# Loading k ahead of q, and the weights in column halves, in a channel-attention plus maxout kernel

## The chip, the cores and the metric

The kernel runs on one core of one Trainium2 chip. The metric is the device time of one execution in microseconds (us). Each kernel was run several times; a "run" below is one execution. All runs quoted here are of the state called fast (none is marked slow in the record). The profile is a trace of one execution; its span is about 1.8 us shorter than the run time of that execution.

The engines: PE is TensorE (matmul), PEld its weight loads, DVE is VectorE, ACT is ScalarE, POOL issues the loads that cast, SP issues the stores.

## The reference

Four batches. In each, a 256 x 256 attention matrix is formed between channels, over 6144 tokens, and the result goes through a maxout layer:

```python
# q, k, v: [4, 6144, 256] fp32, tau = 1
qn = q / (norm(q, axis=1) + 1e-6);  kn = k / (norm(k, axis=1) + 1e-6)   # norms over the tokens
a  = softmax(kn.transpose(0, 2, 1) @ qn / tau)                          # [4, 256, 256]
x  = (v @ a).reshape(24576, 256)
h  = maximum(maximum(x @ w1, x @ w2), x @ w3)                           # w: [256, 768]
out = h @ w_out                                                         # [24576, 256] fp32
```

The kernel never forms v @ a. It folds the attention matrix into the weights (A^T W, a [256, 768] matrix for each of w1 to w3 and each batch) and multiplies v by that.

## The kernel before

Per batch: *gram* multiplies q by k, and also q by q and k by k, whose diagonals are the squared norms; *softmax_t* makes `et`, the unnormalised exponentials; *rowsums* and *aw_half* make A^T W in two column halves; then 12 chunks of 512 tokens follow, each of six blocks (three matmul pairs, then a maximum over the three results by ACT and DVE) and four output steps. Batch b+1's gram stands before the last chunk of batch b, its softmax after the first block (block 0) of that chunk.

```python
alloc_qk(0)
for w in [2, 2] + [4] * 10 + [2, 2]:          # batch 0: q and k alternate, fp32 -> fp8 on the way
    load_qk(0, g0, w); g0 += w                # a piece of width w is w*256 values on each of 128 partitions
for i, w in enumerate(w_list):                # then w1, w2, w3 whole, v(0), v(1), w_out, v(2)
    ...
def gram(b):                                  # one pass over q and k
    ps = [xtile(f"gram{j}") for j in range(CC)]           # CC = 2
    for tp in range(NG // 2):                             # 24 steps
        for j in range(CC):
            PE.matmul(ps[j][:, 0:C],           lhsT=q_j, rhs=k, ...)       # fp8 DoubleRow
            PE.matmul(ps[j][:, C:C + P],       lhsT=q_j, rhs=q_j, ...)
            PE.matmul(ps[j][:, C + P:C + 2*P], lhsT=k_j, rhs=k_j, ...)
    return ps
def softmax_t(ps):
    dkm = ps's k.k blocks * identity                      # DVE, 2 instructions
    PE.matmul(kb_ps, lhsT=ones_f, rhs=dkm)                # k's norms, to all partitions, fp32
    n2q = diagonal sums of ps's q.q blocks                # DVE
    lnk, rkb = Ln(kb_ps), Exp(-0.5 * lnk)                 # ACT: 1 / norm of k
    lnq, rq  = Ln(n2q), Exp(-0.5 * lnq)                   # ACT: 1 / norm of q
    for j in range(CC):
        e_in = ps[j][:, 0:C] * rkb                        # DVE
        et[:, j, :] = Exp(e_in * rq[:, j])                # ACT
...
aw_half(et, rinv, aw, 0); v_transpose(0); aw_half(et, rinv, aw, 1)    # batch 0, ahead of chunk 0
```

(`htile` takes one of six PSUM buffers, which the blocks use too; `xtile` one of two, for gram, transposes and output.)

## Time and profile before

| | before |
|---|---|
| median of the first runs | 631.12 us (630.97 to 632.14) |
| the profiled execution | 629.19 us, span 627.3 us |
| PE busy | 598.0 us, 95% |
| q and k of batch 0 all landed | 36.6 us |

The table of engines on the page of the kernel before (busy us, share of the span, instructions):

```profile
PE 598.0 (95%) x3960; PEld 371.3 (59%) x3960; DVE 409.9 (65%) x638; ACT 287.6 (46%) x529; POOL 69.8 (11%) x134
```

PE is nearly always busy, so time can only be won where PE waits or does needless work. The view of waits, for PE alone (who waited for whom: us in total, times, longest), says where it waits:

```profile
PE gram L148 <- DMA k_sb<-in_k_dram: 14.8, 12, 5.2
PE kb_ps L163 <- DVE dkm L160: 5.9, 4, 1.8
...
PE h_ps L240 <- ACT s_mx L243: 0.8, 3, 0.3
PE vt_ps L226 <- DMA v_sb<-in_v_dram: 0.5, 1, 0.5
```

The 14.8 us are the loading of batch 0. The kb_ps wait is the softmax: one of 0.4 us at the start and one of 1.8 us at each of three batch boundaries. Both places are seen in the timeline (start us, length us, engine, line, operation, out<-in, count, and in brackets the idle time before it and what ended that). This is the start, from the landing of the last k; rows of weight loads and a few others are left out:

```profile
36.59 0.27 PE L148 MATMUL gram<-k_sb,q_sb 128*128 128x512 fp8e4 x1 [0.26 <-DMA k_sb<-in_k_dram]
...
37.09 0.49 DVE L160 TENSOR_TENSOR dkm<-gram,ident 128x128 f32<-128x128 f32 x2 [36.08 <-PE gram L152]
...
37.63 0.70 PE L163 MATMUL kb_ps<-dkm,ones_f 128*128 128x256 f32 x2 [0.41 <-DVE dkm L160]
...
38.37 0.38 ACT L171 ACTIVATE lnk<-kb_ps 128x256 f32<-128x256 f32 x1 [36.35 <-PE kb_ps L163]
...
39.23 0.75 DVE L180 TENSOR_TENSOR e_in<-gram,rkb 128x256 f32<-128x256 f32 x2 [1.11 <-ACT rkb L172]
...
39.76 0.91 ACT L181 ACTIVATE et<-e_in,rq 128x256 bf16<-128x256 f32 x2 [0.23 <-DVE e_in L180]
...
40.81 2.17 PE L205 MATMUL ew_ps<-w_sb,et 128*128 128x384 bf16 x12
```

From the landing at 36.59 us to the first ew_ps matmul at 40.81 (A^T W) there are 4.2 us of a chain that runs through DVE, PE, ACT, DVE and ACT again. Later, v_transpose of chunk 1, which stands between blocks 0 and 1, began at 47.18 us. The next lines are PE at the first batch boundary. The gram before them began at 162.28:

```profile
174.26 1.47 PE L240 MATMUL h_ps<-vt_sb,aw_sb 128*128 128x512 bf16 x6
177.56 0.67 PE L163 MATMUL kb_ps<-dkm,ones_f 128*128 128x256 f32 x2 [1.83 <-DVE dkm L160]
...
181.09 1.51 PE L240 MATMUL h_ps<-vt_sb,aw_sb 128*128 128x512 bf16 x6 [0.27 <-ACT s_mx L243]
182.44 0.82 PE L259 MATMUL o_ps<-wo_sb,ht_sb 128*128 128x256 bf16 x6
```

Block 0 of the last chunk (6 matmuls) is followed by a wait of 1.83 us for dkm, then kb_ps, then blocks 1 and 2 (left out), a wait of 0.27, block 3, and at 182.44 an output step. From 174.26 to 182.44 PE does 5.2 us of block matmuls (24 at 0.216) in 8.18 us.

The view of windows gives, for a stretch, PE busy, granted clock, the busy share of the DMA engines and the GB/s written:

```profile
3.00:10.00 7.00, 2.06 (x12) 1.00 1.05 77
12.00:28.00 16.00, 12.51 (x80) 1.00 1.12 105
```

The DMA engines are full. (Their share is a mean over 16 engines and reads above 1 in both stretches, so the GB/s say more about the speed.) Since fp32 becomes fp8, 105 GB/s written is about 420 GB/s read (an estimate, 4 x 105).

### The profile page before, as it was taken

Reading aid. Unit: us, or ns where it says so; the run is one execution under the profiler, and the core shown is the slowest. Engines: PE = TensorE matmul, PEld = TensorE weight load, DVE = VectorE, ACT = ScalarE, POOL = GpSimd, SP = SyncE. Lnnn points to the kernel's source line nnn. Section 1 sums busy time; section 2 is a strip of 40 time slices with the busy share of each in tenths; the row PEclk is TensorE's granted clock in tenths of the full one; section 3 lists DMA queues with packets and bytes.
Section 4 is the critical chain, followed back from the end, with each engine's and each line's share of the span. In section 5 each row is a group of like instructions: output and inputs, shape, how many; then the busy total and the mean of one; then the engine's idle time right before and its main releaser. Section 6 shows DMA issues by size and latency. Waiting matters only on the chain. (4 is left out here: it accounts for less than half of the span.)

```text
span 627.3 us, 10335 instructions
## 1 busy us (share of the span) xinstructions
PE 598.0 (95%) x3960; PEld 371.3 (59%) x3960; DVE 409.9 (65%) x638; ACT 287.6 (46%) x529; POOL 69.8 (11%) x134
## 2 busy tenths in 40 slices
PE   3779999999989999999989999999998999999996
PEld 3755555555855555555676555555585555565554
DVE  0038777777366877777716877777736677777774
ACT  0045554555146555454416554454514655545452
POOL 6432111100002212100001211110000000000000
PEclk9999999999999999999999999999999999999999
DMA  8999676513009676722204857652300431311011
GB/s 72 105 182 131 116 107 117 96 51 102 35 1 150 99 97 121 106 86 67 85 1 71 122 111 109 119 94 59 93 34 1 101 69 50 100 53 68 35 67 68
DMA packets 26418, 52.58 MB, mean 84 GB/s; under 512 B 2816, under 2 KB 14080, under 8 KB 26368
## 3 DMA queue, kind: packets, MB, share of 16 engines
q0 software_dynamic: 19456, 26.75, 36.4%
q1 hardware_dynamic: 6912, 25.17, 10.2%
q8 instruction: 31, 0.51, 0.3%
q14 instruction: 19, 0.16, 0.1%
HBM read 78.64 MB, written 25.17 MB: 165 GB/s over the span
## 5 line engine op out<-in xcount | busy, mean ns | idle before, releaser
L240 PE MATMUL h_ps<-vt_sb,aw_sb 128*128 128x512 bf16 x1728 | 410.2, 379 | 0.8 <-ACT s_mx L243 0.8
L244 DVE TENSOR_TENSOR s_mx<-h_ps,s_mx 128x512 bf16<-128x512 f32 x288 | 197.9, 687 | 130.5 <-ACT s_mx L243 130.5
L240 PEld LDWEIGHTS <-aw_sb 128*128 128x128 bf16 x1728 | 167.0, 98 | 157.0 <-issue 2.2
L243 ACT ACTIVATE s_mx<-h_ps 128x512 bf16<-128x512 f32 x288 | 171.4, 596 | 162.4 <-PE h_ps L240 162.4
L245 DVE TENSOR_TENSOR ht_sb<-h_ps,s_mx 128x512 bf16<-128x512 f32 x288 | 199.3, 692 | 30.0
L259 PE MATMUL o_ps<-wo_sb,ht_sb 128*128 128x256 bf16 x1152 | 155.4, 273 | 0.9 <-DVE ht_sb L245 0.9
L259 PEld LDWEIGHTS <-ht_sb 128*128 128x128 bf16 x1152 | 112.7, 98 | 51.9 <-DVE ht_sb L245 1.1
L262 ACT ACTIVATE o_sb<-o_ps 128x512 f32<-128x512 f32 x96 | 57.3, 597 | 91.4 <-PE o_ps L259 88.8
L108 POOL DMA_DIRECT2D v_sb<-in_v_dram x48 | 25.7, 535 | 469.5 <-PE vt_ps L226 366.3
L148 PE MATMUL gram<-k_sb,q_sb 128*128 128x512 fp8e4 x192 | 55.7, 327 | 14.8 <-DMA k_sb<-in_k_dram 14.8
L229 ACT ACTIVATE vt_sb<-vt_ps 128x512 bf16<-128x512 bf16 x96 | 52.1, 594 | 34.8 <-PE vt_ps L226 34.8
L152 PE MATMUL gram<-k_sb 128*128 128x256 fp8e4 x192 | 46.6, 243 | 0.0
L150 PE MATMUL gram<-q_sb 128*128 128x256 fp8e4 x192 | 46.2, 241 | 0.0
L150 PEld LDWEIGHTS <-q_sb 128*128 128x256 fp8e4 x192 | 27.8, 145 | 9.6 <-issue 9.3
L226 PEld LDWEIGHTS <-v_sb 128*128 128x128 bf16 x384 | 25.4, 98 | 11.3 <-DMA v_sb<-in_v_dram 0.9
L148 PEld LDWEIGHTS <-q_sb 128*128 128x256 fp8e4 x192 | 27.7, 144 | 6.3 <-DMA q_sb<-in_q_dram 5.9
L152 PEld LDWEIGHTS <-k_sb 128*128 128x256 fp8e4 x192 | 30.2, 157 | 0.0
L226 PE MATMUL vt_ps<-ident,v_sb 128*128 128x128 bf16 x384 | 29.3, 219 | 0.5 <-DMA v_sb<-in_v_dram 0.5
L160 DVE TENSOR_TENSOR dkm<-gram,ident 128x128 f32<-128x128 f32 x8 | 1.9, 281 | 36.1 <-PE gram L152 36.1
L171 ACT ACTIVATE lnk<-kb_ps 128x256 f32<-128x256 f32 x4 | 1.5, 384 | 44.6 <-PE kb_ps L163 44.6
L100 POOL DMA_DIRECT2D k_sb<-in_k_dram x38 | 20.8, 548 | 9.6 <-DMA k_sb<-in_k_dram 7.2
L99 POOL DMA_DIRECT2D q_sb<-in_q_dram x38 | 20.7, 544 | 6.2 <-DMA q_sb<-in_q_dram 6.1
(27 smaller groups left out, 78.4 us busy)
## 6 DMA issues: line engine op xcount, KB each, us to landing
out_dram<-o_sb SPq DMA_DIRECT2D x48, 512.0 KB, 2.6
v_sb<-in_v_dram POOLq DMA_DIRECT2D x48, 256.0 KB, 3.6
q_sb<-in_q_dram POOLq DMA_DIRECT2D x24, 192.0 KB, 5.4
k_sb<-in_k_dram POOLq DMA_DIRECT2D x24, 192.0 KB, 6.9
q_sb<-in_q_dram POOLq DMA_DIRECT2D x10, 128.0 KB, 9.7
k_sb<-in_k_dram POOLq DMA_DIRECT2D x10, 128.0 KB, 9.7
w_sb<-in_moe_w_dram POOLq DMA_DIRECT2D x3, 384.0 KB, 8.0
wo_sb<-in_moe_w_out_dram POOLq DMA_DIRECT2D x1, 384.0 KB, 11.2
```

The source lines that it names most:

```text
L108: POOL.dma_start(out=t, in_=v_r[gi // NCH, gi % NCH])
L148: PE.matmul(ps[j][:, 0:C], lhsT=qt[:, tsl, jsl], rhs=kt[:, tsl, :], start=(tp == 0), stop=last, perf_mode=DR, skip_group_check=True)
L150: PE.matmul(ps[j][:, C:C + P], lhsT=qt[:, tsl, jsl], rhs=qt[:, tsl, jsl], start=False, stop=last, perf_mode=DR, skip_group_check=True)
L152: PE.matmul(ps[j][:, C + P:C + 2 * P], lhsT=kt[:, tsl, jsl], rhs=kt[:, tsl, jsl], start=False, stop=last, perf_mode=DR, skip_group_check=True)
L226: PE.matmul(vt_ps[:, i * P:(i + 1) * P], lhsT=v_sb[:, t, cc * P:(cc + 1) * P], rhs=ident, is_transpose=True, start=(i == 0), stop=(i == CC ...
L229: ACT.activation(out=vt[:, cc, :], in_=vt_ps[:, cc * CHUNK:(cc + 1) * CHUNK], func=AF.Copy)
L240: PE.matmul(t, lhsT=aw[m][:, ic, fsl], rhs=vt[:, ic, :], start=(ic == 0), stop=(ic == CC - 1))
L243: ACT.activation(out=s_mx, in_=hp[0], func=AF.Copy)
L244: DVE.tensor_tensor(out=s_mx, in0=hp[1], in1=s_mx, op=ALU.max)
L245: DVE.tensor_tensor(out=ht[:, fc, :], in0=hp[2], in1=s_mx, op=ALU.max)
L259: PE.matmul(st["ps"][:, half], lhsT=ht[:, fc, t * P:(t + 1) * P], rhs=wo_sb[:, fc, :], start=(fc == 0), stop=(fc == FC - 1))
L262: ACT.activation(out=st["o"][:, t - 1:t + 1, :].rearrange("p t d -> p (t d)"), in_=st["ps"], func=AF.Copy)
```

## The change

The intent: k's norms need only k. If k is loaded whole ahead of q, k.k and its whole chain (dkm, kb_ps, lnk, rkb) run while q is still arriving, and only q's norms are left when the last q lands. Weights come in halves, so that the first half of A^T W can start sooner, and v(0) comes between the halves; the second half of A^T W moves behind block 0 of chunk 0. The gram function is shared, so later batches change too: the k.k pass comes first, and dkm, kb_ps, lnk, rkb run inside gram.

```diff
-    for w in [2, 2] + [4] * 10 + [2, 2]:
-        load_qk(0, g0, w)
+    for load, widths in ((load_k, [4, 4] + [8] * 5), (load_q, [8] * 5 + [4, 2, 2])):
+        ...  # the identity is made after the second k piece instead of before the first
-    (w1, w2, w3 whole), load_v(0), load_v(1)
+    load_w(0); load_v(0); load_w(1); load_v(1)          # column halves
 def gram(b):
+        kk = htile("kk")
+        for tp in range(NG // 2):
+            for j in range(CC):
+                PE.matmul(kk[:, jsl], lhsT=k_j, rhs=k_j, ...)
+        dkm = kk * identity                              # DVE
         for tp in range(NG // 2):
             for j in range(CC):
                 PE.matmul(q_j, k) ; PE.matmul(q_j, q_j)
-                PE.matmul(k_j, k_j)
+            if tp == 11:
+                kb_ps (PE), lnk, rkb (ACT)
-def softmax_t(ps):      # dkm, kb_ps, n2q, lnk, rkb, lnq, rq, e_in, et
+def softmax_t(ps, rkb): # n2q, lnq, rq, e_in, et
...
     v_transpose(0)
-    aw_half(et, rinv, aw, 1)
...
+            if gi == 0:
+                gaps[0].insert(0, lambda: aw_half(et, rinv, aw, 1))   # after block 0 of chunk 0
```

More of the change, by code (lines that the diff above doesn't have):

```diff
@@ L95, in alloc_qk, with load_k, load_q @@
                  qk_pool.tile([P, NG, C], FP8, name="k_sb", tag="k"))
-    def load_qk(b, g0, w):
-        qt, kt = qk[b]
-        POOL.dma_start(out=qt[:, g0:g0 + w, :], in_=q_r[b][:, g0:g0 + w, :])
-        POOL.dma_start(out=kt[:, g0:g0 + w, :], in_=k_r[b][:, g0:g0 + w, :])
+    def load_k(b, g0, w):
+        POOL.dma_start(out=qk[b][1][:, g0:g0 + w, :], in_=k_r[b][:, g0:g0 + w, :])
+    def load_q(b, g0, w):
+        POOL.dma_start(out=qk[b][0][:, g0:g0 + w, :], in_=q_r[b][:, g0:g0 + w, :])
     v_tiles = {}
@@ L109, in load_v, with load_w @@
         v_tiles[gi] = t
-    ident = consts.tile([P, P], BF16, name="ident")
-    make_identity(nc, ident)
     alloc_qk(0)
-    g0 = 0
-    for w in [2, 2] + [4] * 10 + [2, 2]:
-        load_qk(0, g0, w)
-        g0 += w
-    w_sb = []
-    for i, w in enumerate(w_list):
-        wt = consts.tile([P, CC, d_ff], BF16, name=f"w{i}_sb")
-        POOL.dma_start(out=wt, in_=w.rearrange("(cc p) f -> p cc f", p=P))
-        w_sb.append(wt)
+    for load, widths in ((load_k, [4, 4] + [8] * 5), (load_q, [8] * 5 + [4, 2, 2])):
+        g0 = 0
+        for w in widths:
+            load(0, g0, w)
+            g0 += w
+            if load is load_k and g0 == 8:
+                ident = consts.tile([P, P], BF16, name="ident")
+                make_identity(nc, ident)
+    w_sb = [consts.tile([P, CC, d_ff], BF16, name=f"w{i}_sb") for i in range(3)]
+    def load_w(fh):
+        fsl = slice(fh * FH, (fh + 1) * FH)
+        for wt, w in zip(w_sb, w_list):
+            POOL.dma_start(out=wt[:, :, fsl], in_=w.rearrange("(cc p) f -> p cc f", p=P)[:, :, fsl])
+    load_w(0)
     load_v(0)
+    load_w(1)
     load_v(1)
@@ L141, in gram @@
         qt, kt = qk[b]
+        kk = htile("kk")
+        for tp in range(NG // 2):
+            tsl = slice(2 * tp, 2 * tp + 2)
+            for j in range(CC):
+                jsl = slice(j * P, (j + 1) * P)
+                PE.matmul(kk[:, jsl], lhsT=kt[:, tsl, jsl], rhs=kt[:, tsl, jsl], start=(tp == 0 and j == 0),
+                          stop=(tp == NG // 2 - 1), perf_mode=DR, skip_group_check=True)
+        dkm = sm.tile([P, C], FP32, name="dkm")
+        for j in range(CC):
+            jsl = slice(j * P, (j + 1) * P)
+            DVE.tensor_tensor(out=dkm[:, jsl], in0=kk[:, jsl], in1=ident, op=ALU.mult)
         ps = [xtile(f"gram{j}") for j in range(CC)]
@@ L151, in gram @@
                           start=False, stop=last, perf_mode=DR, skip_group_check=True)
-                PE.matmul(ps[j][:, C + P:C + 2 * P], lhsT=kt[:, tsl, jsl], rhs=kt[:, tsl, jsl],
-                          start=False, stop=last, perf_mode=DR, skip_group_check=True)
-        return ps
-    def softmax_t(ps):
-        dkm = sm.tile([P, C], FP32, name="dkm")
-        for j in range(CC):
-            DVE.tensor_tensor(out=dkm[:, j * P:(j + 1) * P], in0=ps[j][:, C + P:C + 2 * P],
-                              in1=ident, op=ALU.mult)
-        kb_ps = htile("kb_ps")
-        PE.matmul(kb_ps[:, :C], lhsT=ones_f, rhs=dkm, start=True, stop=True)
+            if tp == 11:
+                kb_ps = htile("kb_ps")
+                PE.matmul(kb_ps[:, :C], lhsT=ones_f, rhs=dkm, start=True, stop=True)
+                lnk = sm.tile([P, C], FP32, name="lnk")
+                rkb = sm.tile([P, C], FP32, name="rkb")
+                ACT.activation(out=lnk, in_=kb_ps[:, :C], func=AF.Ln)
+                ACT.activation(out=rkb, in_=lnk, func=AF.Exp, scale=-0.5)
+        return ps, rkb
+    def softmax_t(ps, rkb):
         n2q = sm.tile([P, CC], FP32, name="n2q")
@@ L168, in softmax_t @@
                                      op0=ALU.mult, op1=ALU.add, accum_out=n2q[:, j:j + 1])
-        lnk = sm.tile([P, C], FP32, name="lnk")
-        rkb = sm.tile([P, C], FP32, name="rkb")
-        ACT.activation(out=lnk, in_=kb_ps[:, :C], func=AF.Ln)
-        ACT.activation(out=rkb, in_=lnk, func=AF.Exp, scale=-0.5)
         lnq = sm.tile([P, CC], FP32, name="lnq")
@@ L268, in o_steps @@
         return [lambda t=t: step(t) for t in range(TPC)]
-    ps = gram(0)
-    et = softmax_t(ps)
+    et = softmax_t(*gram(0))
     aw = alloc_aw()
@@ L288 @@
             if more and 1 <= ch < 9:
-                load_qk(b + 1, (ch - 1) * 6, 6)
+                load_k(b + 1, (ch - 1) * 6, 6)
+                load_q(b + 1, (ch - 1) * 6, 6)
             gaps = [[] for _ in range(FC)]
@@ L301 @@
                 if ch == NCH - 1 and more and fc == 0:
-                    et = softmax_t(ps)
+                    et = softmax_t(*ps)
                 for f in gaps[fc]:
```

## The prediction

> **What bounds the kernel now.** TensorE. Engine table: PE busy 598 of 627.3 us (95%), DVE 65%, ACT 46%. The waits view lists only about 25 us for PE, nearly all in two places: 14.8 us for k_sb while batch 0's q and k arrive (0 to 37 us), and each batch's softmax: 5.9 us for dkm before the kb_ps matmul (0.4 us at the start, 1.8 us at each of three batch boundaries), 2.2 us for et, 0.5 us for v_sb. So the change can only act on the start and three boundaries.
>
> **The start** is bound by DMA: from 12 to 28 us the windows view shows 104 to 105 GB/s written with the engines full. Fp32 becomes fp8, so about 418 GB/s is read (estimate)[...]. The bytes are the same, so k ahead of q doesn't shorten the stream. It ends earlier because the identity is no longer ahead of the first issue (1.42 us, to about 0.75: 0.7 us), and perhaps because the 2-wide pieces leave the front, where only about 80 GB/s was written from 3 to 10 us (estimate 0 to 1 us). The last k lands at 36.6 us; I expect the last q at about 35.4.
>
> After that landing, the timeline before shows: gram's end, dkm 37.1, kb_ps 37.6, lnk 38.4, rkb to 39.2, e_in, et from 39.8, first ew_ps 40.8, h_ps of block 0 from 45.9 to 47.2: landing + 10.6. After, dkm to rkb are done during q's arrival; left are n2q (0.6), lnq, rq (0.4), et: ew_ps at landing + 2.7 instead of + 4.2. v(0) lands before the second weight half, so the 0.5 us wait goes. But the second half of A^T W, moved behind block 0, no longer fills PE during the vt_sb copies (1.08 us on ACT): 0.7 to 1 us comes back as a new wait of h_ps for vt_sb. Block 0 plus both halves end at about landing + 9.8. Start in all: 1.2 + 0.8 = 2.0 us.
>
> PE clock: triples of gram matmuls took 0.44 us until 35.6 us, then 0.25[...].
>
> **Each boundary.** Gram has the same 144 matmuls and weight loads. The 1.8 us dkm wait goes, and lnk/rkb (0.8 us) leave ACT's chain. But the next blocks' PSUM then waits for ACT, which runs et before s_mx: from block 0 to the end of block 3 I work out 6.6 us instead of 8.2. kb_ps (0.5) moves into gram. Net 0.9 us each, 2.7 in all; gram could grow by 0.5 us each where weight loads bind (0.08 us apart, warm).
>
> **Prediction.** 631.1 - 2.0 - 2.7 = 626.4 us; 8 in 10 between 623.0 and 629.2. Faster by over 2%: 0.02; within 2%: 0.97; slower: 0.01.
>
> **Shown right or wrong by:** last q landing near 35.4; ew_ps near landing + 2.7; a new h_ps wait for vt_sb; at boundaries no dkm wait but an h_ps wait for s_mx of 1.4 us instead of 0.3; gram at 12 us per batch.
>
> **Wrong if:** PE is cold and behind q; wide pieces stream faster or slower; the kk pass is bound by weight loads; DVE is late with dkm.

Two passages are cut, and the cuts are marked. Neither held a term of the sum, which stands as recorded: 631.1 - 2.0 - 2.7 = 626.4 us. One compared the estimated 418 GB/s with a figure that no run of this case shows; the other explained the change from 0.44 to 0.25 us, and expected from that explanation that PE would keep up with q; no run of this case shows it. "Cold" and "warm" are only names for the wider and the closer spacing of gram's matmuls.

## The result, and the profile after

| | before | after |
|---|---|---|
| median | 631.05 us (630.47 to 632.14, 4 runs) | 624.96 us (624.64 to 625.25, 4 runs) |
| ratio, with 95% interval | | 0.9901 (0.9884 to 0.9919) |
| the profiled execution: run time, span | 629.19, 627.3 | 624.64, 622.8 |

A ratio here is the mean time of one kernel's fast runs over that of the other's of the same rounds, so it is not quite the ratio of the medians.

The change gains 1%, about 6.1 us by the medians; that is clear of the noise. But the two profiles differ by only 4.5 us. That gap is itself a finding, taken up below.

PE's waits after the change:

```profile
PE kk L154 <- DMA k_sb<-in_k_dram: 13.7, 7, 5.2
PE h_ps L253 <- ACT s_mx L256: 3.5, 3, 1.2
PE gram L166 <- DMA q_sb<-in_q_dram: 2.5, 3, 1.2
...
PE h_ps L253 <- ACT vt_sb L242: 0.7, 1, 0.7
```

The dkm wait is gone, as intended. In its place stand a wait of h_ps for s_mx, about 1.2 us at each of the three boundaries, and one of 0.7 us for vt_sb at the start. The start after the change, from the landing of the last q (rows left out as before):

```profile
35.04 0.32 PE L166 MATMUL gram<-k_sb,q_sb 128*128 128x512 fp8e4 x1
...
36.12 0.75 DVE L193 TENSOR_TENSOR e_in<-gram,rkb 128x256 f32<-128x256 f32 x2
...
36.70 0.91 ACT L194 ACTIVATE et<-e_in,rq 128x256 bf16<-128x256 f32 x2
...
37.77 3.62 PE L218 MATMUL ew_ps<-w_sb,et 128*128 128x384 bf16 x12
...
42.52 1.73 PE L253 MATMUL h_ps<-vt_sb,aw_sb 128*128 128x512 bf16 x5 [0.69 <-ACT vt_sb L242]
...
44.08 2.11 PE L218 MATMUL ew_ps<-w_sb,et 128*128 128x384 bf16 x12
...
46.03 0.61 PE L239 MATMUL vt_ps<-ident,v_sb 128*128 128x128 bf16 x8
```

The last q lands at 35.04 us instead of 36.59, and the first ew_ps starts 2.73 us after it instead of 4.2. So far, that is 3.0 us won. But then 12 ew_ps matmuls take 3.62 us, where they took 2.17 before. The windows view (columns as above: PE busy with its count, granted clock, DMA share, GB/s) shows why:

```profile
36.00:37.00 1.00, 0.00 (x0) 1.00 1.32 212
...
37.40:37.60 0.20, 0.04 (x1) 0.61 1.06 196
37.60:40.60 3.00, 2.94 (x12) 0.50 1.26 199
```

PE idled from 35.6 to 37.27 us, and from about 37.4 to 40.9 us its granted clock was 0.50. The mark, v_transpose of chunk 1 (the last line of the timeline above), is at 46.03 us, only 1.15 us earlier than before; it now has block 0 and all of A^T W behind it, as it had before. What halved the clock this profile alone doesn't show; experiment 3 tests the idle gap before it, and experiments 2 and 4 show that the outcome changes from run to run.

At the first boundary, where gram began at 161.13 us:

```profile
173.81 3.83 PE L253 MATMUL h_ps<-vt_sb,aw_sb 128*128 128x512 bf16 x17
178.83 1.51 PE L253 MATMUL h_ps<-vt_sb,aw_sb 128*128 128x512 bf16 x6 [1.18 <-ACT s_mx L256]
180.18 0.82 PE L272 MATMUL o_ps<-wo_sb,ht_sb 128*128 128x256 bf16 x6
```

Blocks 0 to 2 run in one piece (the trace has 17 of their 18 matmuls), and block 3 waits 1.18 us. Blocks 0 to 3 now take 6.37 us (173.81 to 180.18) instead of 8.18. Gram takes 12.68 us instead of 11.98, mostly since kb_ps is inside it. From the start of gram to the end of block 3 it is 19.05 instead of 20.16 us: 1.11 us less. The other two boundaries show the same (19.04 instead of 20.16, 19.05 instead of 20.15), so the three give 3.3 us.

The stream of loads:

```profile
3.00:10.00 7.00, 1.49 (x8) 1.00 1.03 87
12.00:28.00 16.00, 10.40 (x69) 1.00 1.06 107
```

It moves 2% more per us once it runs, and more in its first 7 us, in which the kernel before issued four 2-wide pieces.

(The trace of the changed kernel's first profile lacks 63 of the 1728 block matmuls, so its PE busy time is not compared.)

### The profile page after: what moved, and what is told of

It reads as the page before. It is cut to its first block, busy times and chain, and to the rows that moved or that the text cites. A ratio compares the mean times of both kernels' runs of the same rounds, so it can differ in the third digit from the quotient of the medians.

```text
span 622.8 us, 10260 instructions
## 1 busy us (share of the span) xinstructions
PE 592.0 (95%) x3897; PEld 366.8 (59%) x3960; DVE 410.2 (66%) x638; ACT 288.5 (46%) x529; POOL 64.9 (10%) x124
## 5 line engine op out<-in xcount | busy, mean ns | idle before, releaser
L253 PE MATMUL h_ps<-vt_sb,aw_sb 128*128 128x512 bf16 x1665 | 404.8, 379 | 7.7 <-ACT s_mx L256 3.5
L166 PE MATMUL gram<-k_sb,q_sb 128*128 128x512 fp8e4 x192 | 36.3, 290 | 2.5 <-DMA q_sb<-in_q_dram 2.5
L168 PE MATMUL gram<-q_sb 128*128 128x256 fp8e4 x192 | 34.7, 226 | 0.0
L154 PE MATMUL kk<-k_sb 128*128 128x256 fp8e4 x192 | 20.0, 269 | 13.7 <-DMA k_sb<-in_k_dram 13.7
L166 PEld LDWEIGHTS <-q_sb 128*128 128x256 fp8e4 x192 | 27.4, 142 | 3.6 <-DMA q_sb<-in_q_dram 3.5
L154 PEld LDWEIGHTS <-k_sb 128*128 128x256 fp8e4 x192 | 18.1, 146 | 15.4 <-DMA k_sb<-in_k_dram 14.8
L168 PEld LDWEIGHTS <-q_sb 128*128 128x256 fp8e4 x192 | 26.3, 137 | 0.2
L159 DVE TENSOR_TENSOR dkm<-kk,ident 128x128 f32<-128x128 f32 x8 | 2.0, 285 | 27.8 <-PE kk L154 27.8
L224 DVE TENSOR_SCALAR aw_sb<-ew_ps,rinv 128x384 bf16<-128x384 f32 x24 | 14.6, 617 | 8.0 <-PE ew_ps L218 7.6
L101 POOL DMA_DIRECT2D q_sb<-in_q_dram x32 | 17.6, 553 | 11.1 <-DMA k_sb<-in_k_dram 11.1
```

The costliest lines, as they stand in the source:

```text
L154: PE.matmul(kk[:, jsl], lhsT=kt[:, tsl, jsl], rhs=kt[:, tsl, jsl], start=(tp == 0 and j == 0), stop=(tp == NG // 2 - 1), perf_mode=DR, ski ...
L166: PE.matmul(ps[j][:, 0:C], lhsT=qt[:, tsl, jsl], rhs=kt[:, tsl, :], start=(tp == 0), stop=last, perf_mode=DR, skip_group_check=True)
L168: PE.matmul(ps[j][:, C:C + P], lhsT=qt[:, tsl, jsl], rhs=qt[:, tsl, jsl], start=False, stop=last, perf_mode=DR, skip_group_check=True)
L253: PE.matmul(t, lhsT=aw[m][:, ic, fsl], rhs=vt[:, ic, :], start=(ic == 0), stop=(ic == CC - 1))
```

## The experiments

Each was run against the kernel before on the same chip; kernels of one group share those runs. The groups (experiments 1, 2, 3 and 8; 4 to 7; 9 to 11) ran on three different chips, so small differences between medians of different groups are to be read with care. All gave correct results.

### 1. The boundaries alone

Edit: the start of the kernel before (loads, weights, one-pass gram for batch 0, both halves of A^T W ahead of chunk 0); later batches as changed.

```diff
-    et = softmax_t(*gram(0))
+    et = softmax_t(*gram_joint(0))        # the one-pass gram of before; loads and weights as before
```

> The start of the kernel before (q and k alternating, whole weights, one pass over q and k for batch 0), the two-pass gram only for batches 1 to 3. Theory (the gain is about 1.1 us at the start and 1.1 us at each of three boundaries): 3.4 us below before, about 627.7 us, with block 0 of batch 0 at the same time as before (h_ps near 45.9 us). Rival (the gain comes from the start, as the change's words suggest): the same as before, 631.

Measured: 627.33 us median (626.99 to 627.83, 5 runs), before 630.74 (11 runs), ratio 0.9948 (0.9936 to 0.9959). That is 3.3 us, by the ratio: more than half of the whole gain is at the three boundaries, where no load was waited for. The rival (all from the start) falls. Its trace also shows that the start of the kernel before can meet the halved clock (0.50 from 42 to 44 us):

```profile
37.25 0.44 PE L182 MATMUL gram<-k_sb,q_sb 128*128 128x512 fp8e4 x1
...
41.46 3.62 PE L250 MATMUL ew_ps<-w_sb,et 128*128 128x384 bf16 x12
...
48.60 0.61 PE L271 MATMUL vt_ps<-ident,v_sb 128*128 128x128 bf16 x8
```

The same trace shows a second way in which this start can be slow. Its gram triples (q.k, q.q, k.k) start 0.44 us apart up to the last one, at 37.25 us, so that PE ends gram behind the loads; in the profile of the kernel before, the spacing fell to about 0.24 us at 35.7 us, and PE waited for the last k. With both, ew_ps begins 0.65 us later than in that profile, and the mark comes at 48.60 instead of 47.18 us. In the first profile of the changed kernel the pairs of gram matmuls go from 0.32 to 0.17 us apart at 27.2 us, 4.5 us into a stretch of q matmuls without a wait (22.63 to 28.93 us), and in all ten traces with the changed start they are 0.17 us apart by 35 us; with q and k alternating, PE waited for a load 12 times in the profile of before. Why the spacing falls, and whether k ahead of q has a part in it, is not shown: no run changes the order of the loads alone.

### 2. The start alone

Edit: the changed start, with the one-pass gram and late k norms of before for batches 1 to 3.

```diff
-                ps = gram(b + 1)
+                ps = gram_joint(b + 1)    # dkm, kb_ps, lnk, rkb again in softmax_t
```

> The changed start, with the one-pass gram of before for batches 1 to 3 (dkm, kb_ps, lnk and rkb in the next chunk again). Theory: only the start's 1.1 us, about 629.9 us, with the 1.8 us wait for dkm back at each boundary; this gain and that of the boundaries-only run add up to the whole 6 us of run time within 1 us or so. Rival: nearly the whole gain, about 625.

Measured: 627.83 us median (626.89 to 628.69, 6 runs), ratio 0.9952 (0.994 to 0.9965): about 3.0 us, not the expected 1.1. The wait of the boundaries is back, as it should be:

```profile
PE kb_ps L202 <- DVE dkm L199: 5.5, 3, 1.8
```

The six runs are two groups: 626.89, 627.07, 627.20 with a mean granted clock of 0.999 to 1.000, and 628.46, 628.61, 628.69 with 0.996. The expectation of 1.1 us came from subtracting one profile from the other, and the one of the kernel before is of an execution (629.19 us) faster than all 11 runs of before of this experiment (629.26 to 631.27), while that of the changed kernel had the halved clock. The two parts add up: 3.3 + 3.0 = 6.3 us, against 6.2 for the whole by its ratio. The 3.0 us also fit the traces once the one of experiment 1 stands for the start of before: its mark at 48.60 us is 2.6 us after that of the changed kernel with the halved clock (46.03) and 3.7 after the one without it (44.95, experiment 4), and half of the six runs are of either kind.

### 3. PE kept busy during the softmax of batch 0

```diff
-    et = softmax_t(*gram(0))
+    ps, rkb = gram(0)
+    warm = htile("warm")                  # nobody reads it
+    for i in range(14):
+        PE.matmul(warm[:, 0:C], lhsT=q[:, 0:2, 0:P], rhs=k[:, 0:2, :], ...)
+    et = softmax_t(ps, rkb)
```

> The changed kernel with 14 more DoubleRow matmuls into a PSUM tile that nobody reads, between batch 0's gram and its row sums, where PE idles 1.7 us. Theory: PE's clock fell to half from 37.4 to 40.9 us because of that idle time, and the 12 ew_ps matmuls took 3.6 us instead of 2.1; kept busy, the clock stays at 1.00, ew_ps takes 2.1 us and the kernel is 1.4 us faster than the changed one (about 623.6). Rival: the arrival of v(0) and of the second weight half would hold PE then anyway: clock 1.00, but less than 0.5 us gained. Other rival: the clock does not depend on this idle time, and still falls.

Measured: 623.53 us median (623.43 to 624.06, 4 runs, clock 0.999 or more in all), ratio 0.9889. PE in its trace:

```profile
35.89 1.70 PE L287 MATMUL warm<-k_sb,q_sb 128*128 128x512 fp8e4 x14
...
38.22 2.11 PE L218 MATMUL ew_ps<-w_sb,et 128*128 128x384 bf16 x12
```

ew_ps takes 2.11 us again. Idle matmuls, which do nothing for the result, save 1.4 us against the 624.96 of the changed kernel's first session. That is a comparison across sessions, but the two groups of experiment 2, on the same chip as this one, lie 1.5 us apart. The count of runs is clearer still: of the 30 runs with the changed start and no idle matmuls (the first four of the changed kernel, and experiments 2, 4, 6, 7 and 8), 20 have a mean clock of 0.994 to 0.997; of the 17 with them (3 and 9 to 11), none is below 0.999. So both rivals fall. The idle matmuls make no execution faster than the best of the changed kernel (next experiment); they take away its slower ones.

### 4. The changed kernel once more

No edit.

> The changed kernel unaltered, again, to compare within one session and to see the spread of its runs. Theory: its runs fall in two groups, with the clock dropped during batch 0's ew_ps (624.6 to 625.3 us, mean granted clock 0.996) and not dropped (about 623.5, clock 0.999 or more), and nothing between. Rival: one group, with the times of the first four runs.

Measured: 623.65 us median (623.03 to 627.03, 6 runs), before 630.12 (11 runs), ratio 0.9907 (0.9884 to 0.9929). Four runs are at 623.03 to 623.73 with a clock of 0.999 or more, one at 625.46 with 0.996, and one at 627.03 with 0.994, which the expected two groups don't explain. This time the profile fell on an execution without the halving (span 621.8 us; clock 1.00 in every us from 36 to 44, after the same gap of 1.68 us before the row sums, and with PE busy 3% from 36 to 37), so it can be laid beside the profile of before like for like. PE:

```profile
35.48 0.32 PE L166 MATMUL gram<-k_sb,q_sb 128*128 128x512 fp8e4 x1
...
38.20 2.11 PE L218 MATMUL ew_ps<-w_sb,et 128*128 128x384 bf16 x12
...
44.95 0.61 PE L239 MATMUL vt_ps<-ident,v_sb 128*128 128x128 bf16 x8
```

The last q landed at 35.48 us (the landing moves by some tenths from run to run), and the mark, v_transpose of chunk 1, came at 44.95, against 47.18 before: 2.2 us at the start. With 3.3 us at the boundaries that is about 5.5 us, and the spans differ by 627.3 - 621.8 = 5.5 us.

### 5. PE kept busy in the kernel before

```diff
         PE.matmul(kb_ps[:, :C], lhsT=ones_f, rhs=dkm, start=True, stop=True)
+        if warm:                          # batch 0 only, 16 matmuls into an unread PSUM tile
+            for i in range(warm): PE.matmul(wm[:, 0:C], ...)
```

> The kernel before with 16 idle DoubleRow matmuls into an unread PSUM tile after batch 0's kb_ps, where its PE idles for 2 us. Theory: the same coin is tossed in the kernel before; its profile (run of 629.2 us) is one without the drop, its median (631) one with it. Kept busy, all runs lie near 629.3, 1.4 us below the median of before, and the change against this kernel still gains what the start and the boundaries give. Rival: before's spread has another cause, and the median stays near 631.

Measured: 629.45 us median (628.78 to 629.61, 6 runs); before 630.12 (628.70 to 632.58, 11 runs); ratio 0.9984 (0.9966 to 1.0001). The spread shrank and the time is where it was expected, but the interval touches 1, and the mean clock of a run doesn't sort the runs of before into two groups. Its trace, like that of experiment 1, has the gram triples 0.44 us apart to the last (36.98 us), which matmuls put in after gram can't change. So it stays open how much of the spread of before is the halving and how much the slow gram; experiment 1 shows only that its start can meet both. Mean clocks of 0.981 to 0.992 occur only in runs with the start of before. No such run was profiled and they are not consistently slower than others, so what they stand for is open too.

### 6. Narrow pieces

```diff
-((load_k, [4, 4] + [8] * 5), (load_q, [8] * 5 + [4, 2, 2]))
+((load_k, [2, 2] + [4] * 11), (load_q, [4] * 11 + [2, 2]))
```

> The changed kernel with k and q of batch 0 in pieces of 4 (2 at the two ends) instead of 8, in the same order. Theory: the wider pieces gave part of the earlier end of the stream (107 instead of 104.5 GB/s written over 30 us: about 0.7 us); with narrow ones the last q lands at about 35.7 instead of 35.0 us, and the kernel is 0.5 to 1 us slower than the changed one. Rival: the earlier end comes from issuing 0.7 us sooner alone: 35.0 us, no change.

Measured: 625.54 us median (624.82 to 626.47, 6 runs). The windows view shows 81 GB/s from 3 to 10 us and 104 from 12 to 28, against 87 and 107 with wide pieces, and the last q landed at about 36.1 us, against 35.04 and 35.48 in the two profiles of the changed kernel. Five of these runs have a clock of 0.996 or 0.997 and a mean of 625.60 us; the five runs of the changed kernel with 0.996, from two sessions, have a mean of 625.06. So narrow pieces cost about 0.5 us, with the caution that a session differs; the one narrow run at 0.999, 624.82, lies 1.1 us or more above the four of the changed kernel at that clock in the same session. The first load is issued at 1.23 us with narrow and with wide pieces (1.42 in the kernel before), and in all nine traces with wide pieces PE had the last q by 35.6 us. So the width of the pieces, not only the earlier first issue, brought the landing forward, and the rival falls: the earlier issue is 0.2 us, not 0.7. An 8-wide piece writes 256 KB and a 4-wide one 128 KB (the DMA view); in a queue that is always full (DMA share 1.06 and 1.12 from 12 to 28 us) the difference between 107 and 104 GB/s is about 3%.

### 7. DVE's half of the softmax ahead of block 0

Edit: for batches 1 to 3, n2q and e_in are issued right after gram, when DVE has nothing to do; lnq, rq and et stay after block 0.

```diff
-                ps = gram(b + 1)
+                part = softmax_dve(*gram(b + 1))     # n2q, e_in
...
-                    et = softmax_t(*ps)
+                    et = softmax_act(*part)          # lnq, rq, et
```

> The changed kernel with DVE's half of each later batch's softmax (n2q and e_in) issued right after gram, ahead of block 0's maxima, ACT's half staying where it is. Theory: the 1.2 us wait of h_ps for s_mx at each boundary, which the change got in exchange for the dkm wait, comes from ACT waiting for n2q and e_in behind block 0's DVE work; it goes, and the kernel is about 3 to 4 us faster than the changed one (about 621.3). Rival: the wait is PSUM pressure from DVE's total work in these blocks, and moves elsewhere: less than 1 us gained.

Measured: 621.02 us median (620.67 to 621.23, 4 runs, all with a clock of 0.997), ratio 0.9853. Its trace has the halved clock too (0.50 from 39 to 41 us), and its median is 4.0 us below the mean of the changed kernel's runs at 0.996. The traces agree: from the start of gram to the end of block 3 the first boundary takes 17.64 us here and 19.05 in the changed kernel, 1.4 us less. The h_ps wait for s_mx is no longer listed. ACT at the first boundary, in the changed kernel:

```profile
174.23 0.60 ACT L256 ACTIVATE s_mx<-h_ps 128x512 bf16<-128x512 f32 x1 [3.63 <-PE h_ps L253]
176.92 0.20 ACT L188 ACTIVATE lnq<-n2q 128x2 f32<-128x2 f32 x1 [2.09 <-DVE n2q L184]
...
177.39 0.91 ACT L194 ACTIVATE et<-e_in,rq 128x256 bf16<-128x256 f32 x2
178.20 1.06 ACT L256 ACTIVATE s_mx<-h_ps 128x512 bf16<-128x512 f32 x2
```

and in this one:

```profile
175.02 0.60 ACT L262 ACTIVATE s_mx<-h_ps 128x512 bf16<-128x512 f32 x1 [3.63 <-PE h_ps L259]
175.52 0.20 ACT L196 ACTIVATE lnq<-n2q 128x2 f32<-128x2 f32 x1
...
175.98 0.91 ACT L200 ACTIVATE et<-e_in,rq 128x256 bf16<-128x256 f32 x2
176.79 0.58 ACT L262 ACTIVATE s_mx<-h_ps 128x512 bf16<-128x512 f32 x1
```

In the first, ACT stood still for 2.09 us before lnq, until DVE had finished block 0's two maxima and n2q; s_mx of block 1 came at 178.20, 4 us after that of block 0, and its PSUM was free only then. In the second it comes at 176.79, 1.8 us after, and PE runs 24 block matmuls without a gap. The wait was a matter of order, not of total work.

### 8. The second half of A^T W back ahead of chunk 0

```diff
     v_transpose(0)
+    aw_half(et, rinv, aw, 1)
...
-            if gi == 0:
-                gaps[0].insert(0, lambda: aw_half(et, rinv, aw, 1))
```

> The changed kernel with the second half of A^T W put back ahead of chunk 0 (as before), weights still loaded in halves. Theory: the move is no gain: it opened a 0.7 us wait of h_ps for vt_sb, which those matmuls used to fill; put back, that wait goes and batch 0 is 0.3 to 0.8 us earlier (about 624.4). Rival (the intent of the change): put back, PE waits for the second weight half and the kernel is 0.5 to 1.5 us slower.

Measured: 623.44 us median (623.33 to 624.73, 4 runs). The two runs with a clock of 0.999 or more took 623.33, about what the changed kernel takes at that clock (623.03 to 623.73); of the two at 0.997, one took 624.73 and the other 623.55, less than the changed kernel's 624.64 to 625.25 at 0.996. The profile is of that one:

```profile
37.66 3.69 PE L218 MATMUL ew_ps<-w_sb,et 128*128 128x384 bf16 x12
...
43.68 1.46 PE L253 MATMUL h_ps<-vt_sb,aw_sb 128*128 128x512 bf16 x5
44.98 0.61 PE L239 MATMUL vt_ps<-ident,v_sb 128*128 128x128 bf16 x8
```

With the first half delayed by the clock (0.50 from 39 to 41 us), the second half follows the transposes with no wait, block 0 comes at 43.68, and the mark at 44.98, where it was 46.03 in the changed kernel's first profile. The rival (a wait for the weights) falls here, but this one is not clean: the states differ between the runs. The next two redo it with the clock held up.

### 9 and 10. Everything together, with the half moved and with it put back

The first has the edits of experiments 3 and 7, and the output steps of the last chunk spread over blocks 1 to 4. The second is the same with the edit of experiment 8.

```diff
-                place = [3, 4, 4, 5]
+                place = [1, 2, 3, 4]
```

> A version meant to beat both: the changed kernel with DVE's half of the softmax right after gram, with the 14 idle matmuls that keep the clock up, and with the output steps of each batch's last chunk spread over blocks 1 to 4 (possible now, since gram's PSUM is free earlier). Theory: the two gains add, 621.0 - 1.4 = 619.6, clock 0.999 or more, no h_ps wait for s_mx; the spreading changes nothing, because PE has no wait left there. Rival: they do not add.

> The same, with the second half of A^T W put back ahead of chunk 0. With the half clock that move back gained about 1 us, since the delayed first half hid the arrival of the second. Theory: at full clock PE comes sooner and meets the arriving weights, so little is left: within 0.5 us of the version with the half moved (619.2 to 619.8). Rival: the 0.7 us wait for vt_sb is saved in full: 618.8.

Measured: 619.27 us median (619.06 to 619.55, 5 runs), ratio 0.9817 (0.9803 to 0.983); and 618.88 us (618.77 to 619.15, 4 runs), ratio 0.9812 (0.9798 to 0.9825). The gains add. Putting the half back is worth 0.4 us: the wait for vt_sb (0.7 us) goes, and part of it returns as a wait for the weights. The median lies just under the range of the theory, nearer to the rival's 618.8, though the wait for the weights shows that not all of the 0.7 us is saved. PE's waits in the second kernel have

```profile
PE ew_ps L224 <- DMA w_sb<-in_moe_w_dram: 0.2, 1, 0.2
```

So the move of the second half into the first chunk cost a little instead of gaining. What the spreading of the output steps did was not run by itself.

### 11. Weights whole

Edit: the kernel of experiment 10, with weights loaded whole ahead of v(0), as in the kernel before.

```diff
-    load_w(0); load_v(0); load_w(1); load_v(1)
+    for wt, w in zip(w_sb, w_list): POOL.dma_start(out=wt, in_=w...)
+    load_v(0); load_v(1)
```

> The same as the version with the half put back, but weights loaded whole ahead of v(0), as in the kernel before. Theory: ew_ps now starts about 2.7 us after the last q lands, but the third whole weight lands about 5.6 us after it (2.36 MB at 418 GB/s, an estimate) and v(0) 1.3 us later, so PE waits for DMA and batch 0's block 0 is 1 to 1.5 us later: about 620.5. This is what the split of the weights is worth once the softmax is short. Rival: the split is worth nothing.

Measured: 620.50 us median (620.26 to 620.66, 4 runs), 1.6 us slower than with halves. PE now waits:

```profile
PE ew_ps L224 <- DMA w_sb<-in_moe_w_dram: 1.1, 1, 1.1
...
PE vt_ps L245 <- DMA v_sb<-in_v_dram: 0.4, 1, 0.4
```

1.07 us for the third weight and 0.4 for v(0). With the softmax shortened, the split of the weights is needed; this rival falls.

## Why the prediction was right, point by point

The prediction was 626.4 us, 623.0 to 629.2; measured were 624.96 and, in a second session, 623.65 us.

- *The total.* A gain of 4.7 us was foretold; by the ratio it is 6.2. Both terms were sized low. That 624.96 came within 1.5 us of the forecast is in part luck. The forecast set waits read from an execution of 629.19 us against a median of 631, and did not foresee the halved clock; the first made the gain larger than worked out, the second made it smaller.
- *The start, "2.0 us".* Like for like (both profiles without the halved clock) it is 2.2 us; over the runs of experiment 2, about 3.0, since the profile of before shows a fast start: in the other two traces of that start (experiments 1 and 5) gram ends later. The last q lands at 35.04 and 35.48 us in two profiles ("near 35.4"), though not for the reasons in their given sizes: the first load was issued at 1.23 us and not at 0.75, so the identity gave 0.2 us instead of 0.7, and much of the rest came from the wider pieces (experiment 6), for which it had allowed 0 to 1 us; ew_ps starts 2.73 us later ("near landing + 2.7"), the new h_ps wait for vt_sb is 0.7 us ("0.7 to 1"), and block 0 and both halves are done 9.5 us after the landing without the halving ("+ 9.8"), 11.0 with it.
- *The clock.* The sum has no term for a PE that lags behind q, and none was needed: pairs of gram matmuls started 0.32 us apart until 27 us and 0.17 from 28, and PE waited for the last q. The granted clock reads 1.00 in every window up to 37 us, at both spacings, so it doesn't show that change; the spacing of the matmuls does. What the forecast missed is that the clock can fall to 0.50 after the gap that the softmax leaves, and that the profile of before was of an execution faster than most. The two numbers that tell it, 629.19 us for the profiled run and 631.12 for the median, were there to be seen.
- *Each boundary, "0.9 us each".* Measured 1.11 each in the profiles, 3.3 us in all in experiment 1. Blocks 0 to 3 took 6.37 us ("6.6"), and gram grew by 0.70 us, of which it had put down 0.5 to kb_ps; the separate k.k pass costs about 0.2 us; its matmuls start 0.08 us apart, as those of gram did before. The 0.5 us of growth that it thought possible from weight loads did not come. The wait of h_ps for s_mx came as foretold, at 1.2 instead of 1.4 us, and experiment 7 shows its cause to be the one given: ACT, held by et behind DVE.
- *"Gram at 12 us per batch"* left its own kb_ps out; it is 12.7.

## What to carry to other kernels

A function that is shared by a start and by later rounds changes both: more than half of this gain came from three places where PE waited for no load, because a chain over three engines had moved under gram's own matmuls. When a wait on PE goes, look which engine is next in line for the same buffers: here the dkm wait of 1.8 us turned in part into an s_mx wait of 1.2 us, and issuing 1.4 us of DVE work one block earlier took that away for another 4 us. Before you subtract two profiles, hold the run times of the profiled executions beside the medians and read the clock of the stretch: an idle gap of 1.7 us on PE was here followed, in some executions, by a clock of 0.50 (for 3.4 us in the first profile of the changed kernel; 20 of 30 runs have a mean clock of 0.994 to 0.997), and with 14 matmuls in the gap that nobody reads the mean clock was 0.999 or more in all 17 runs.
